# A fused attention, cosine feed-forward and soft mixture kernel: the logits' steps emitted between a slot's remainder and its cosine

## The chip, the cores and the metric

The kernel runs on one core of a Trainium2 chip. The metric is the time of one execution on the device in microseconds (us), the median of several runs. A profile is one execution recorded by the hardware profiler; its span runs from the first to the last instruction. PE is the matrix engine, PEld its weight loads, DVE the vector engine, ACT the scalar engine, POOL and SP the two engines that here mostly issue DMAs.

## The reference

Three layers follow each other on 4608 tokens of width 512. Only the second and third matter here.

```python
def _moe_ref(x, w_in, w_out):            # x: 4608 x 512, w_in: 512 x 2048
    h = x @ w_in
    g = h * np.cos(h)
    return (g @ w_out).astype(np.float32)

def _moe2_ref(x, phi, w1, w2):           # phi: 512 x 32 slots
    logits = x @ phi
    d = logits - logits.max(0, keepdims=True)
    d = np.exp(d)
    d /= d.sum(0, keepdims=True) + 1e-09
    slot_input = d.T @ x
    ...
    c = logits - logits.max(1, keepdims=True)
    c = np.exp(c)
    c /= c.sum(1, keepdims=True) + 1e-09
    return (c @ slot_out).astype(np.float32)
```

Ahead of this stands a linear attention (a product of k and v for each head, its product with q, and a normalization by the root mean square); its output is x.

## The kernel before, in words

The tokens are cut into ten blocks: blocks 0 to 7 have 512 tokens, blocks 8 and 9 have 256. `SMALL` is 8, `NB` is 10. The 2048 columns of `w_in` are cut into 16 pieces of 128, so a block has 16 slots, written (j, f). From block 8 on, two slots are worked as a pair.

A slot makes one tile of g = h cos h. `main` (L384) issues twelve matmuls (the operands are split into a high and a low part; three products of four pieces each) into one PSUM tile of the pool `ps_m`, which has three tiles. `cos_a` (L405) finds the turns on ACT (L410) and the remainder on DVE (L413). `cos_b` (L430) is the sine on ACT (L417), shifted to a cosine. `cos_c` (L446) multiplies it with h on DVE (L456), which is the last reader of the PSUM tile, and transposes the result on DVE (L475, or L463 in a pair) for the blocks whose slot products use DMA to regroup the rows (`regroup`, L508: DMAs issued by SP and POOL).

The first `w_out` product is never made: the logits come from g and the product of `w_out` and `phi`. `logits` (L523, matmuls L528) adds four slots at a time into one PSUM tile. Over the tokens, a running maximum and a running sum are kept, and A is the running sum of exponentials times g. For block j the steps are, in their order:

- the last `logits`, then `l_evac` (L545): the logits are copied from PSUM by DVE (L547);
- `l_add` (L550): four small matmuls spread them over the partitions (L555);
- `l_max` (L569): the maximum (L573) and a scaling (L574) on DVE, and the copy of the logits into a tile `ld` (L576);
- `l_cross` (L583): a matmul (L585) brings the maxima of the partitions together, and DVE takes their maximum (L586) and the new running maximum (`l_new`, L589: L592, L593, L595, L596);
- `l_exp` (L598): the exponentials on ACT into `ld` (L602), with their sum; the factor for the old sum (L611); the running sum on DVE (L612);
- `l_T` (L621): two transposes on PE, first of the exponentials, then of the copied logits (L629), and two copies by DVE (L631, L632);
- `slot_acc` (L654) and `slot_add` (L669): 16 matmuls d times g (L665), added to A on DVE (L674).

The order of everything is written out by hand. `PLAN` gives each step a slot. `at` puts a step in `side` (run behind `main` of that slot), `late` in `post` (behind `cos_a`), `end` in `fin` (behind `cos_c`), `ld_at` in `loads` (ahead of `main`). Steps in `amid` are run inside `main`, behind the fourth matmul (behind the eighth in block 8). Each engine works through its own instructions in the order of emission. `U(j, f)` turns a slot past 15 into one of the next block. For blocks 2 to 6 the last `logits` and `l_evac` are in slot 17 of block j, that is (j+1, 1), `l_add` and `l_max` in (j+1, 2), `l_cross` and `l_exp` inside `main` of (j+1, 3), `l_T` behind `main` of (j+1, 4) and `slot_acc` in (j+1, 6). For block 7 they are in (8, 1), (8, 2), (8, 3), (8, 5) and (8, 7). For block 0 `l_evac` is in (1, 14), `l_add` in (1, 15), `l_cross` in (2, 0); for block 1 they are in (2, 2), (2, 3) and (2, 4), with `l_T` in (2, 5) and `slot_acc` in (2, 6).

The loop from L1183 runs a slot as `loads`, `main`, `side`, `cos_a`, `post`, `cos_b`, `cos_c`, `fin`; the loop from L1192 does the same for pairs.

Of the kernel before, what the change touches and what calls it, by code (L numbers as in the profile page):

```python
# [8 lines left out]
F32 = mybir.dt.float32  # L9
# [17 lines left out]
    wq=(7, 10, 13, 15),  # L27
    l0=(9, 9, 12, 13, 15, 15, 17, 17),
    E=((18, 19, 3, 1), (18, 19, 3, 1)),
    F=((21, 22), (21, 22)),  # L30
    L=4,
    LI=2,
    PI=2,
# [11 lines left out]
    le=17,  # L45
    la=18,
# [18 lines left out]
NB = len(SIZES)  # L65
# [3 lines left out]
SMALL = SIZES.index(256)  # L69
# [3 lines left out]
def tile_linear_attention__ffn_cos__soft_moe(  # L73
# [13 lines left out]
    nc = tc.nc  # L87
    B, H, D = kv.shape[0], 8, 64
    NF, KD = w_in.shape[0], w_in.shape[2]
# [14 lines left out]
    ps_m = ctx.enter_context(tc.tile_pool(name="ps_m", bufs=PLAN["pm"], space=bass.MemoryType.PSUM))  # L104
# [279 lines left out]
    def main(j, f, ps=None):  # L384
        if ps is None:
            ps = ps_m.tile([128, 512], F32, tag="h", name="h")
        w, x = w_t[f], xt_t[j]
        assert all((j, t) in x_done for t in range(TT[j])) and ("S", f, 0) in done
        n = 0
        for kk in range(KD):  # L390
            for a, b in ((0, 0), (0, 1), (1, 0)):
                nc.tensor.matmul(out=ps, lhsT=w[:, a, kk, :], rhs=x[b][:, kk, :],  # L392
                                 start=(n == 0), stop=(n == 3 * KD - 1))
                n += 1
                if n == (8 if j == SMALL else 4):
                    run(amid, j, f)
        h_t[j, f] = ps

# [31 lines left out]
    def cos_b(j, f):  # L430
        cosine(fr_t[j, f])
# [86 lines left out]
                    in_=src[32 * x:32 * x + 32].rearrange("p (t b) f i -> p b t (f i)", b=4)[:, b],  # L518
                )

    l_t = {}

    def logits(j, c):  # L523
        if c == 0:
# [44 lines left out]
    def l_max(j):  # L569
        ps = lr_t[j]  # L570
        mb = sm_p.tile([128, 8], F32, tag="mb", name="mb")
        if j < SMALL:
            nc.vector.tensor_reduce(out=mb[:, 0:1], in_=ps[:, 0:128], axis=AX.X, op=ALU.max)  # L573
            nc.vector.tensor_scalar(out=mb[:, 4:8], in0=quarter, scalar1=mb[:, 0:1], scalar2=None, op0=ALU.mult)  # L574
            ld = one_p.tile([128, TB], F32, tag="ls", name="ld").rearrange("p (i t) -> p i t", t=128)[:, 0:2]
            nc.vector.tensor_copy(out=ld[:, 0], in_=ps[:, 0:128])  # L576
            lr_t[j] = (ps, mb, ld)
        else:
            nc.vector.tensor_reduce(out=mb[:, 0:1], in_=ps, axis=AX.X, op=ALU.max)
            lr_t[j] = (ps, mb, None)  # L580
            l_new(j)
# [16 lines left out]
    def l_exp(j):  # L598
        ps, mb, ld = lr_t.pop(j)
        sb = sm_p.tile([128, 2], F32, tag="sb", name="sb")  # L600
        if j < SMALL:
            nc.scalar.activation(out=ld[:, 1], in_=ps[:, 0:128], func=AF.Exp, bias=mb[:, 2:3], accum_out=sb[:, 0:1])  # L602
        else:
            ld = one_p.tile([128, TB], F32, tag="ls", name="ld")[:, 0:SIZES[j]]
            nc.scalar.activation(out=ld, in_=ps, func=AF.Exp, bias=mb[:, 2:3], accum_out=sb[:, 0:1])
            if j == NB - 1:
                ls_t[j] = ps
            else:
                nc.vector.tensor_copy(out=ld[0:32], in_=ps[0:32])
        if j:  # L610
            nc.scalar.activation(out=mb[:, 3:4], in_=mb[:, 1:2], func=AF.Exp)  # L611
            nc.vector.scalar_tensor_tensor(out=s_run, in0=s_run, scalar=mb[:, 3:4], in1=sb[:, 0:1],  # L612
                                           op0=ALU.mult, op1=ALU.add)
        else:
            nc.vector.tensor_copy(out=s_run, in_=sb[:, 0:1])
        ld_t[j] = ld
        sc_t[j] = mb

    ab_t = {}

# [307 lines left out]
    side = {}  # L928
# [6 lines left out]
    def late(j, f, fn, *a):  # L935
        post.setdefault((j, f), []).append((fn, a))
# [3 lines left out]
    def U(j, f):  # L940
        if j == 0 and f >= NF:
            j, f = 1, f - L
        return j + f // NF, f % NF
# [4 lines left out]
    def late2(j, f, *a):  # L948
        late(*U(j, f), *a)

    fin, amid = {}, {}

    def end(j, f, fn, *a):
        fin.setdefault((j, f), []).append((fn, a))
# [9 lines left out]
    for j in range(NB):  # L964
# [26 lines left out]
        if j < NB - 1:  # L991
            for c in range(4 * (j > 1)):
                at2(j, 4 * c + 7 if j == SMALL else PLAN["lg"][c], logits, j, c)
            le, la, lx, how = (PLAN["E"][j] if j < 2 else (19, 21, 5, 1) if j == SMALL
                               else (PLAN["le"], PLAN["la"], *PLAN["lx"]))
            at2(j, le, l_evac, j)
            at2(j, la, l_add, j)
            at2(j, la, l_max, j)
            if j < SMALL:
                amid.setdefault(U(j, la + 1), []).extend([(l_cross, (j,)), (l_exp, (j,))])  # L1000
            else:
                (at2, late2, end2)[how](j, NF + lx, l_exp, j)
        else:
            for c in range(3):
                at2(j, (7, 11, 14)[c], logits, j, c)
            at2(j, 14, l_evac, j)
            at2(j, 15, l_add, j)
            for f in range(12, NF):
                side.setdefault((j + (f + 2) // NF, (f + 2) % NF if f > 13 else 15), []).insert(0 if f > 13 else 99, (l_add, (j, f)))
            at2(j, 18, l_max, j)  # L1010
            at2(j, 18, warm, 5)
            end(NB, 3, l_exp, j)
            side[NB, 0].insert(0, (exp_table, ()))
# [43 lines left out]
    def run(d, j, f):  # L1057
        for fn, a in d.pop((j, f), []):
            fn(*a)

    wo2 = {}

# [93 lines left out]
    with tc.manual_schedule():  # L1156
# [24 lines left out]
            for t in (PLAN["one"] if f < L else PLAN["two"]).split():  # L1181
                token(t, f)
        for j, f in [(1, f) for f in range(NF - L, NF)] + [(j, f) for j in range(2, SMALL) for f in range(NF)]:  # L1183
            run(loads, j, f)
            main(j, f)
            run(side, j, f)
            cos_a(j, f)
            run(post, j, f)
            cos_b(j, f)
            cos_c(j, f)  # L1190
            run(fin, j, f)
        for j, f in [(j, f) for j in range(SMALL, NB) for f in range(0, NF, 2)]:  # L1192
            if (j, f) == (NB - 1, NF - 2):
                for i in range(2):
                    ps = ps_m.tile([128, 512], F32, tag="h", name="h")[:, 0:256]
                    run(loads, j, f + i)
                    main(j, f + i, ps)
                    run(side, j, f + i)
                    if i:
                        cos_b(j, f)  # L1200
                    cos_a(j, f + i)
                cos_c(j, f)
                cos_b(j, f + 1)
                cos_c(j, f + 1)
                continue
            ps = ps_m.tile([128, 512], F32, tag="h", name="h")
            for i in range(2):
                run(loads, j, f + i)
                main(j, f + i, ps[:, 256 * i:256 * i + 256])
                run(side, j, f + i)  # L1210
            h_t[j, f] = ps
            cos_a(j, f)
            for i in range(2):
                run(post, j, f + i)
            cos_b(j, f)
            cos_c(j, f)
            for i in range(2):
                run(fin, j, f + i)
# [71 lines left out]
```

## Time and profile before

| what | value |
|---|---|
| median of 3 runs | 674.75 us (673.41 to 674.92) |
| the profiled execution | 675.04 us |
| its span | 673.2 us |
| mean granted clock of PE, of full | 0.994 |
| busy PE, PEld | 643.4 us, 473.6 us |
| busy DVE, ACT, POOL | 492.6 us, 325.1 us, 208.7 us |
| read from and written to memory | 91.29 MB, 13.63 MB |

Busy is the time in which an engine works on an instruction, from the first to the last; matmuls are pipelined, so their modelled ends overlap, and a busy PE need not be at its peak. Time an engine spends waiting is put down to the instruction that ended the wait. An engine that is not the bottleneck may wait without cost.

### The profile page before, as it was taken

The numbers are of one execution on the slowest core, as the hardware profiler recorded it, in microseconds if no ns is written. First come the engines' busy times: TensorE is split into PE (matmuls) and PEld (weight loads), VectorE is DVE, ScalarE is ACT, GpSimd is POOL, SyncE is SP. The second block draws the span as 40 slices with busy tenths as digits, with TensorE's granted clock in tenths as the row PEclk, the third lists the DMA queues.
The fourth block names the chain that finished last, engine by engine and source line by source line (L and its number), as shares of the span: only waits on it lengthen the run. The fifth ranks groups of instructions, "written<-read, shape, count | busy, mean of one in ns | idle before, by whom it ended". The sixth has DMA issues, their size and how long they took to land.

```text
span 673.2 us, 12709 instructions
## 1 busy us (share of the span) xinstructions
PE 643.4 (96%) x4689; PEld 473.6 (70%) x4689; DVE 492.6 (73%) x927; ACT 325.1 (48%) x589; POOL 208.7 (31%) x291
## 2 busy tenths in 40 slices
PE   7889999999999999999999999999999999999993
PEld 6767787776557776777677677767667778984452
DVE  3899989966666778887888788787777756556243
ACT  3576767544344445445444554543463443553032
POOL 2451112310363443542543243335416322200000
PEclk9999999999999999999999999999999999999997
DMA  8955664212385636784788377575745369999998
GB/s 316 362 187 192 203 217 141 63 31 63 89 195 138 173 81 177 199 238 107 182 219 210 93 184 207 160 217 143 166 116 121 68 192 287 310 411 399 407 405 356
DMA packets 70589, 135.13 MB, mean 201 GB/s; under 512 B 10752, under 2 KB 39040, under 8 KB 69504
## 3 DMA queue, kind: packets, MB, share of 16 engines
q1 hardware_dynamic: 63360, 119.63, 55.5%
q0 software_dynamic: 7168, 14.69, 9.6%
q8 instruction: 37, 0.61, 0.4%
q14 instruction: 24, 0.20, 0.1%
HBM read 91.29 MB, written 13.63 MB: 156 GB/s over the span
## 4 chain that ended last, share of the span: by engine, by line
PE 75%; DVE 11%; DMA 5%; ACT 3%; issue 2%; POOL 1%; SPq 1%; DVEq 0%; ACTq 0%
PE h L392 47%; PE ab L665 5%; PE ops L203 4%; PE l L528 3%; DMA g<-tr 2%; DVE tmp L413 2%; PE eh L821 2%; PE eo L858 2%; PE kvps L184 2%; DVE gT L456 2%; DVE tr L475 2%; PE xTps L242 2%; ACT tmp L417 2%; PE l L537 2%; PE tr L497 2%
## 5 line engine op out<-in xcount | busy, mean ns | idle before, releaser
L392 PE MATMUL h<-xt,w 128*128 128x512 f32 (+1 forms) x1920 | 423.1, 374 | 2.4 <-POOL w L328 1.0
L392 PEld LDWEIGHTS h<-xt,w 128*128 128x128 f32 x1920 | 328.7, 189 | 84.2 <-issue 12.9
L417 ACT ACTIVATE tmp<-tmp,hpi 128x512 f32<-128x512 f32 (+1 forms) x145 | 104.2, 720 | 182.4 <-DVE tmp L413 182.2
L516 POOL DMA_DIRECT2D g<-tr x224 | 123.8, 555 | 119.6 <-DVE tr L475 47.1
L456 DVE TENSOR_TENSOR gT<-tmp,h 128x512 f32<-128x512 f32 x130 | 89.2, 686 | 68.3 <-ACT tmp L417 68.2
L217 POOL TENSOR_TENSOR ri<-ss,mhalf 128x8 f32<-128x8 f32 x36 | 59.5, 1656 | 188.1 <-DVE ss L215 178.6
L413 DVE SCALAR_TENSOR_TENSOR tmp<-h,tmp 128x512 f32<-128x512 f32 (+1 forms) x145 | 97.2, 674 | 23.7 <-ACT tmp L410 23.1
L410 ACT ACTIVATE tmp<-h 128x512 int32<-128x512 f32 (+1 forms) x145 | 85.2, 587 | 45.0 <-PE h L392 42.7
L475 DVE STREAM_TRANSPOSE tr<-gT 128x512 f32<-128x512 f32 x103 | 73.2, 711 | 6.9 <-DMA g<-tr 2.2
L328 POOL TENSOR_TENSOR w<-st_m,w 128x512 fp32r<-128x512 f32 x16 | 21.4, 1336 | 63.0 <-ACT w L323 63.0
L203 PE MATMUL ops<-kvA,q 128*128 128x128 f32 (+1 forms) x320 | 38.7, 279 | 0.1
L203 PEld LDWEIGHTS ops<-kvA,q 128*128 128x128 f32 (+1 forms) x320 | 34.5, 180 | 2.9 <-issue 1.9
L246 ACT ACTIVATE xt<-xTps,gn 128x512 fp32r<-128x512 f32 x36 | 24.5, 685 | 21.2 <-PE xTps L242 21.2
L665 PE MATMUL ab<-g,d 128*32 128x512 f32 x256 | 33.2, 593 | 1.4 <-DMA g<-tr 1.4
L528 PE MATMUL l<-gT,wp 128*32 128x512 f32 (+1 forms) x248 | 30.9, 556 | 0.0
L255 DVE SCALAR_TENSOR_TENSOR xt<-xTps,gn,xt 128x512 fp32r<-128x512 f32 x36 | 25.9, 728 | 4.1 <-ACT xt L246 4.0
L212 ACT ACTIVATE sq<-ops 128x512 f32<-128x512 f32 x31 | 18.4, 595 | 18.2 <-PE ops L203 18.2
L214 DVE TENSOR_REDUCE ss<-sq 128x8 f32<-128x512 f32 x31 | 21.1, 679 | 7.6 <-ACT sq L212 7.4
L665 PEld LDWEIGHTS ab<-g,d 128*32 128x32 f32 x256 | 10.0, 110 | 21.0 <-issue 19.1
L224 DVE TENSOR_TENSOR sq<-ops,ri 128x512 f32<-128x512 f32 x31 | 20.9, 676 | 1.2 <-POOL ri L217 1.2
L184 PEld LDWEIGHTS kvps<-kv 128*64 128x64 f32 x448 | 15.4, 137 | 8.7 <-issue 5.2
L242 PE MATMUL xTps<-ident,sq 128*128 128x128 f32 x124 | 18.9, 276 | 1.7 <-DVE sq L224 1.7
(205 smaller groups left out, 596.4 us busy)
## 6 DMA issues: line engine op xcount, KB each, us to landing
kv<-in_kv SPq DMA_DIRECT2D x28, 512.0 KB, 5.4
g<-tr SPq DMA_DIRECT2D x224, 64.0 KB, 4.0
g<-tr POOLq DMA_DIRECT2D x224, 64.0 KB, 4.0
ew<-in_ew SPq DMA_DIRECT2D x23, 512.0 KB, 9.0
q<-in_qT SPq DMA_DIRECT2D x36, 256.0 KB, 6.3
out<-ot SPq DMA_DIRECT2D x11, 768.0 KB, 6.5
rw<-in_w_in SPq DMA_DIRECT2D x16, 512.0 KB, 4.4
nat<-in_w_out SPq DMA_DIRECT2D x16, 512.0 KB, 4.1
```

The costliest lines, as they stand in the source:

```text
L203: nc.tensor.matmul(out=ps[p0:p0 + n, pr * 128:(pr + 1) * 128], lhsT=q_t[j, t][:, pr, p0:p0 + n], rhs=kvbd[b % 2][:, pr, :], start=True, st ...
L217: nc.gpsimd.tensor_tensor(out=ri[:, :, 0], in0=ss, in1=mhalf, op=ALU.pow)
L242: nc.tensor.transpose(ps[:, kk * 128:(kk + 1) * 128], xs[:, kk * 128:(kk + 1) * 128], ident)
L392: nc.tensor.matmul(out=ps, lhsT=w[:, a, kk, :], rhs=x[b][:, kk, :], start=(n == 0), stop=(n == 3 * KD - 1))
L410: nc.scalar.activation(out=t.bitcast(I32), in_=ps, func=AF.Copy, bias=0.25, scale=INV_2PI)
L413: nc.vector.scalar_tensor_tensor(out=t, in0=ps, scalar=INV_2PI, in1=t.bitcast(I32), op0=ALU.mult, op1=ALU.subtract)
L417: nc.scalar.activation(out=t, in_=t, func=AF.Sin, bias=hpi, scale=TWO_PI)
L456: nc.vector.tensor_tensor(out=g, in0=fr, in1=h_t.pop((j, f)), op=ALU.mult)
L475: nc.vector.transpose(out=tr_t[j, q][:, :, i, :], in_=gT_t[j, n * q + i].rearrange("p (b t) -> p b t", t=32))
L516: (nc.gpsimd if b % 2 else nc.sync).dma_start(out=dst[32 * b:32 * b + 32, :, x, a:a + n, :].rearrange("p t f i -> p t (f i)"), in_=src[32 ...
L528: nc.tensor.matmul(out=l_t[j][32 * o:32 * o + 32, :], lhsT=wp[:, f, :], rhs=gT_t.pop((j, f)), start=(c == 0), stop=(c == (2 if j == NB - 1 ...
L665: nc.tensor.matmul(out=ps[32 * c:32 * c + 32, :], lhsT=d[:, t, :], rhs=gs[c // 2][t][:, (c % 2) * 512:(c % 2) * 512 + 512], start=(t == 0) ...
```

## The change

The code of the next slot's `main` is emitted between `cos_a` and `cos_b` of the slot before, together with the logits' steps that belong to that next slot: `go` runs `loads` and `main` of a slot once, `go_next` does so for the slot that `nxt` names and takes the listed steps out of its `side`. For blocks 2 to 6 these are the last `logits` and `l_evac`, then `l_add` and `l_max`; for blocks 0 and 1 only `l_add` and `l_max`. `l_cross` stays inside `main` of the slot behind, now emitted ahead of the earlier slot's `cos_b`; `l_exp` follows that `cos_b`, and the new `l_sum` (the copy of the logits into `ld` and the running sum) follows its `cos_c`. For block 7, whose steps fall into pairs, `l_add` and `l_max` are emitted behind `cos_a` of pair (8, 0), with `main` of (8, 2) into a tile taken early; `l_cross` comes behind the twelfth matmul of `main` (8, 3), `l_exp` behind `cos_a` of pair (8, 2), `l_sum` behind its `cos_c`. `slot_acc` and `slot_add` of block 1 go from (2, 6) to (2, 7).

```diff
-    F=((21, 22), (21, 22)),
+    F=((21, 22), (21, 23)),
...
-                if n == (8 if j == SMALL else 4):
+                if n == (12 if j == SMALL else 4):
                     run(amid, j, f)
...
     def l_max(j):
...
-            nc.vector.tensor_copy(out=ld[:, 0], in_=ps[:, 0:128])
             lr_t[j] = (ps, mb, ld)
...
     def l_exp(j):
...
             if j == NB - 1:
                 ls_t[j] = ps
-            else:
-                nc.vector.tensor_copy(out=ld[0:32], in_=ps[0:32])
         if j:
             nc.scalar.activation(out=mb[:, 3:4], in_=mb[:, 1:2], func=AF.Exp)
+        sc_t[j] = mb
+        ld_t[j] = ld
+        lr_t[j] = (ps, sb)
+        if j >= SMALL:
+            l_sum(j)
+
+    def l_sum(j):
+        ps, sb = lr_t.pop(j)
+        ld, mb = ld_t[j], sc_t[j]
+        if j < SMALL:
+            nc.vector.tensor_copy(out=ld[:, 0], in_=ps[:, 0:128])
+        elif j < NB - 1:
+            nc.vector.tensor_copy(out=ld[0:32], in_=ps[0:32])
+        if j:
             nc.vector.scalar_tensor_tensor(out=s_run, in0=s_run, scalar=mb[:, 3:4], in1=sb[:, 0:1],
                                            op0=ALU.mult, op1=ALU.add)
         else:
             nc.vector.tensor_copy(out=s_run, in_=sb[:, 0:1])
-        ld_t[j] = ld
-        sc_t[j] = mb
...
             if j < SMALL:
-                amid.setdefault(U(j, la + 1), []).extend([(l_cross, (j,)), (l_exp, (j,))])
+                amid[U(j, la + 1)] = [(l_cross, (j,))]
+                e, a, x = (U(j, k) for k in (le, la, la + 1))
+                if j == SMALL - 1:
+                    late(*a, l_exp, j)
+                    end(*a, l_sum, j)
+                    nxt[a[0], a[1] - 2] = (a, j, (l_add, l_max), False)
+                else:
+                    for q, fns in ((e, (logits, l_evac)), (a, (l_add, l_max)), (x, ())):
+                        if q != e or j > 1:
+                            nxt[divmod(q[0] * NF + q[1] - 1, NF)] = (q, j, fns, q == x)
...
+    def go(j, f, ps=None):
+        if (j, f) not in ran:
+            run(loads, j, f)
+            main(j, f, ps)
+            ran.add((j, f))
+
+    def go_next(j, f, ps=None):
+        if (j, f) not in nxt:
+            return None
+        q, b, fns, last = nxt.pop((j, f))
+        go(*q, ps)
+        rest_ = []
+        for fn, a in side.pop(q, []):
+            if fn in fns and a[0] == b:
+                fn(*a)
+            else:
+                rest_.append((fn, a))
+        if rest_:
+            side[q] = rest_
+        return b if last else None
...
-            run(loads, j, f)
-            main(j, f)
+            go(j, f)
             run(side, j, f)
             cos_a(j, f)
             run(post, j, f)
+            b = go_next(j, f)
             cos_b(j, f)
+            if b is not None:
+                l_exp(b)
             cos_c(j, f)
+            if b is not None:
+                l_sum(b)
             run(fin, j, f)
...
-            ps = ps_m.tile([128, 512], F32, tag="h", name="h")
+            ps = pair_ps.pop() if pair_ps else ps_m.tile([128, 512], F32, tag="h", name="h")
             for i in range(2):
-                run(loads, j, f + i)
-                main(j, f + i, ps[:, 256 * i:256 * i + 256])
+                go(j, f + i, ps[:, 256 * i:256 * i + 256])
                 run(side, j, f + i)
             h_t[j, f] = ps
             cos_a(j, f)
             for i in range(2):
                 run(post, j, f + i)
+            if (j, f) in nxt:
+                pair_ps.append(ps_m.tile([128, 512], F32, tag="h", name="h"))
+                go_next(j, f, pair_ps[0][:, 0:256])
             cos_b(j, f)
             cos_c(j, f)
```

## Rows read from the trace of the kernel before

**Rows 1.** The page: busy time, share of the span and instructions of each engine.
```profile
PE 643.4 (96%) x4689; PEld 473.6 (70%) x4689; DVE 492.6 (73%) x927; ACT 325.1 (48%) x589; POOL 208.7 (31%) x291
```
**Rows 2.** Waits of PE: waiting line, releaser, us in total, times, longest.
```profile
PE lr L585 <- DVE ld L576: 3.9, 4, 1.2
...
PE ab L665 <- DMA g<-tr: 1.4, 1, 1.4
...
PE lr L555 <- DVE ls L547: 0.7, 1, 0.7
...
PE ldT L629 <- ACT ld L602: 0.4, 1, 0.4
```
**Rows 3.** Timeline, block 4's steps: start, length, engine, line, operation, [idle before <-releaser].
```profile
367.07 1.18 PE L392 MATMUL h<-xt,w 128*128 128x512 f32 x4
...
368.23 4.81 PE L392 MATMUL h<-xt,w 128*128 128x512 f32 x20
...
370.42 0.69 DVE L456 TENSOR_TENSOR gT<-tmp,h 128x512 f32<-128x512 f32 x1 [0.79 <-ACT tmp L417]
...
373.92 2.33 PE L392 MATMUL h<-xt,w 128*128 128x512 f32 x9
```
**Rows 4.** Timeline, PE around the L585 of block 0.
```profile
160.12 1.20 PE L392 MATMUL h<-xt,w 128*128 128x512 f32 x4
...
162.46 4.84 PE L392 MATMUL h<-xt,w 128*128 128x512 f32 x20
```
**Rows 5.** Timeline, slot products of blocks 0 and 1 and what follows each.
```profile
173.12 3.64 PE L665 MATMUL ab<-g,d 128*32 128x512 f32 x32
...
176.69 1.16 PE L203 MATMUL ops<-kvA,q 128*128 128x128 f32 x8
...
194.20 0.60 PE L665 MATMUL ab<-kv,d 128*32 128x512 f32 x2
...
200.44 5.75 PE L392 MATMUL h<-xt,w 128*128 128x512 f32 x24
```
**Rows 6.** Timeline, block 7's steps in block 8.
```profile
543.40 0.42 PE L555 MATMUL lr<-ls,rep 128*32 128x128 f32 x8
...
543.75 1.21 PE L392 MATMUL h<-xt,w 128*128 128x256 f32 x8
543.96 0.69 DVE L456 TENSOR_TENSOR gT<-tmp,h 128x512 f32<-128x512 f32 x1 [0.79 <-ACT tmp L417]
...
545.39 0.25 DVE L573 TENSOR_REDUCE mb<-lr 128x1 f32<-128x128 f32 x1
...
545.82 0.28 DVE L576 COPY ld<-lr 128x128 f32<-128x128 f32 x1
...
546.58 0.16 DVE L586 TENSOR_REDUCE mb<-lr 128x1 f32<-128x4 f32 x1 [0.48 <-PE lr L585]
...
547.20 1.28 ACT L602 ACT_TABLE_LOAD   x1 [3.27 <-DVE mb L595]
...
548.50 0.37 ACT L602 ACTIVATE ld<-lr,mb 128x128 f32<-128x128 f32 x1
...
548.95 0.59 ACT L410 ACTIVATE tmp<-h 128x512 int32<-128x512 f32 x1
...
549.97 3.12 PE L392 MATMUL h<-xt,w 128*128 128x256 f32 x24
...
551.60 0.69 DVE L456 TENSOR_TENSOR gT<-tmp,h 128x512 f32<-128x512 f32 x1 [1.34 <-ACT tmp L417]
552.32 0.71 DVE L463 STREAM_TRANSPOSE tr<-gT 128x512 f32<-128x512 f32 x1
552.96 0.25 DVE L631 COPY d<-ldT 128x128 f32<-128x128 f32 x1
```
**Rows 7.** Windows of 1 us: length, busy (instructions) per engine, granted clock, DMA share, GB/s.
```profile
663.00:664.00 1.00, 0.00 (x0) 0.00 (x0) 0.00 (x0) 0.00 (x0) 0.00 (x0) 1.00 1.05 436
...
665.00:666.00 1.00, 0.00 (x0) 0.00 (x0) 0.00 (x0) 0.00 (x0) 0.00 (x0) 0.50 1.03 424
```

More of the change, by code (lines that the diff above doesn't have):

```diff
@@ L519, in regroup @@
                 )
-    l_t = {}
+    l_t, pair_ps = {}, []
     def logits(j, c):
@@ L949, in late2 @@
         late(*U(j, f), *a)
-    fin, amid = {}, {}
+    fin, amid, nxt, ran = {}, {}, {}, set()
     def end(j, f, fn, *a):
```

## The prediction, made from these rows alone

> **What bounds the kernel now.** I read the busy shares first: PE is busy for 643.4 of 673.2 us, DVE for 492.6, ACT for 325.1 [rows 1]. PE sets the pace, so only a wait of PE's own is worth anything, and the second view is the list of what PE waited for [rows 2]. Of its idle time the steps named by the change hold four entries: the cross product of the maxima (L585) waits four times for DVE, 3.9 us in all; the slot product (L665) waits once for a regrouping DMA, 1.4 us; the replication of the logits (L555) waits once for DVE, 0.7 us; the transpose of the exponentials (L629) waits once for ACT, 0.4 us. The timeline shows the four L585 waits in blocks 0, 1, 6 and 7; in blocks 2 to 5 PE does not wait there.
>
> The idle entries understate the loss, because the matmuls' ends are modelled. So I price from start to start. In block 4 nothing is disturbed: from the first of four main matmuls to the resumption after L585 it is 368.23 - 367.07 = 1.16 us [rows 3]. In block 0 it is 162.46 - 160.12 = 2.34 us [rows 4]: that wait costs 1.18 us, not the 0.9 that idle time shows. A slot product takes 176.69 - 173.12 = 3.57 us undisturbed; that of block 1 took 200.44 - 194.20 = 6.24 us, so it lost 2.67 us [rows 5].
>
> Why PE waits at L585: its input is the end of a row on DVE. DVE runs about a slot behind PE, and in its order the cosine's multiply (0.69 us) and transpose (0.71 us) of the slot before stand ahead of the maximum, and the copy of the logits (0.28 us) behind it is waited for too; block 7 shows it [rows 6].
>
> **The change, part by part.** *The order on PE* stays: the next slot's main product came next anyway, and the logits' steps stood right behind it. SP and POOL keep their order too: the next slot's loads (regrouping DMAs among them, four issues on each queue per slot) are emitted earlier, but only past the sine, the multiply and the transpose, which put nothing on those queues. So this part moves DVE and, in block 7, ACT.
>
> *Evacuation and maximum ahead of the multiply* (blocks 0 to 6; in 0 and 1 the maximum alone). For the three L585 waits in blocks 0, 1 and 6 the input comes 0.69 + 0.71 + 0.28 = 1.68 us sooner, against a loss of 1.18 each: they go, 3 x 1.18 = 3.5 us. The lower bound is the idle time, 3.9/4 = 0.98 each, 2.9 us. The evacuation before the multiply also takes block 6's L555 wait (0.7 us), and the exponential earlier takes block 3's L629 wait (0.4 us), whose DVE chain comes out about 1 us earlier. The added wait: DVE now holds evacuation, maximum and cross maximum until the next main product has passed, and the multiply, transpose and next remainder queue behind. Who would notice is PE, for the PSUM tile that the multiply frees (three tiles: slot f+3 needs slot f's). In block 4 the multiply of slot 2 starts at 370.42, ends at 371.11, and slot 5's product starts at 373.92, a slack of 2.8 us [rows 3]. DVE also sat idle 0.79 us before that multiply, waiting for the sine; an evacuation or maximum that fits there costs nothing. I take zero; the upper bound is a rival below.
>
> *Copy and running sum behind the transpose.* Blocks 0 to 6 transpose the exponentials a whole main product later, so the copy is hidden by it.
>
> *The second slot product one slot later.* A main product goes in front of it. Block 1's DMA comes out of a chain that starts at block 0's slot product, so it moves up with block 0's 1.18 us, while PE arrives 2 x 1.18 earlier and then spends a main product of at most 2.9 us (24 matmuls take 5.75 [rows 5]). That leaves 0 to 0.4 us of wait; if the DMA does not move at all, 1.5 us. Gain 2.67 less 0.3: 2.4 us, bounds 1.2 and 2.67.
>
> *Block 7* is emitted differently and here I expect a loss. The exponential goes behind the turns of pair (8,2) and ahead of its sine; the copy goes behind that pair's transpose; the L629 transposes stay behind main (8,5), and the second of them needs the copy. From [rows 6]:
> - the replication ends at 543.40 + 0.42 = 543.82; maximum and scaling take 0.43 (545.39 to 545.82), so the multiply of (8,0) starts at 544.25, and from multiply to the next thing after its transpose it is 545.39 - 543.96 = 1.43: 545.68. The cross product, now after twelve matmuls from 543.75, is done by then (eight took 1.21).
> - from the cross maximum to the table load 547.20 - 546.58 = 0.62: 546.30. From that table load to the multiply 551.60 - 547.20 = 4.40, less the turns (0.60) that now stand ahead: 3.80, so the multiply starts at 550.10. It and the transpose take 552.96 - 551.60 = 1.36, the copy 0.28: 551.74.
> - the second transpose follows, and main (8,6) starts about 0.2 later, near 551.95. Before, it started at 549.97 [rows 6].
> So block 7 ends 2.0 us later than before, with its own L585 wait already gone: PE would reach the transposes at about 548.7 and sit there for 3 us. Bounds: 1.8, if the table is loaded while ACT still waits, and 2.6, if nothing overlaps.
>
> One rule speaks against this part. The row shows the table load at 547.20 for 1.28 us and the exponential at 548.50, so a switch costs 1.30 us and two of them lie in the 3.80 [rows 6]. The Trainium skill ("ScalarE: Activation LUTs", What ACT_TABLE_LOAD costs) puts a drain of some 1.38 us beside each load, 2.66 us a switch. By the page block 7 would lose 2.0 + 2.8 = 4.8 us and the whole would come to 672.6 us; the trace shows no such drain, and I go by it.
>
> **The sum.** 3.5 + 0.7 + 0.4 + 2.4 = 7.0 us gained before block 8, 2.0 given back in it: 5.0 us. The profiled execution took 675.04 us, 1.84 more than its span of 673.2, and lies 0.29 above the median of 674.75. I subtract from the median: 669.75, say **669.8 us**. The tail should follow: its transfers fill all DMA engines (share 1.03 and more [rows 7]), but they start when PE frees weight and slot tiles in blocks 8 and 9, so they start 5.0 us earlier as well.
>
> **Rivals.**
> *No loss in block 7.* If the copy is not what the transposes wait for, or DVE reaches it before PE arrives, the 2.0 us stay, and block 7's own L585 wait is gained: 543.75 to 549.97 is 6.22 us for 36 matmuls that take 36 x 3.12/24 = 4.7 and some 0.4 for the cross product, so 1.1 us. 669.8 - 3.1 = 666.7. Against it stands the emission order: the copy is behind a sine that is behind two table loads.
>
> *The waits come back elsewhere.* PE waits for DVE, DMA and ACT by turns [rows 2]; a PE that is earlier may meet the next one, first of all block 1's DMA: with the lower bounds, 2.9 for L585, 1.2 for the slot product, 0.5 of the two small ones, less 2.6 in block 7, 2.0 is left, so 672.7 us, the edge of no change; with only half of that 673.7.
>
> *The tiles come back too late (slower).* Three DVE steps in a row each wait for a main product. It decides from the point at which the multiply of slots 0 to 2 ends more than the 2.8 us of slack later [rows 3]; from there each us is one of PE in every block that has the new order, seven times. An overrun of 1.2 us gives 7 x 1.2 = 8.4: 678.2 us. For it: DVE is at 73% and a slot behind. Against: the evacuation fits into idle time DVE has anyway, and each wait is for something PE finished about when DVE gets there.
>
> *The clock.* Behind PE's last matmul, from 663 to 664, PE had nothing to do and the granted clock was still full; from 665 to 666 it was at half, 1.2 GHz [rows 7]. The 3 us of idle that I expect in block 7 come near to that. If the clock falls there, the two main products behind (3.12 us [rows 6]) take 3.1 us longer, and the slot product and what follows may too: 673 to 676, take 673.5. The Trainium skill ("TensorE: Matmul & The Clock Gate", What's actually happening) also has the engine at half rate after idling; the end of this trace agrees.
>
> *Dearer switches.* If ACT lost about as much again behind each of the two table loads, 1.3 us by the row's own 1.30, the loss in block 7 grows by 2.6: 672.4. The rows speak against it: the exponential starts 0.02 us after the load ends [rows 6]. By the page it would be the 672.6 given above.
>
> **How the numbers follow.** The forecast as argued: 0.60, its own range 668.3 to 671.8. No loss in block 7: 0.08. Waits come back: 0.12. Clock: 0.08. Dearer switches: 0.03. Tiles too late: 0.09. The range leaves out the tiles and most of the no-loss case: 667.0 to 674.0. A measurement of this kernel tells 0.3% from no change, 2.0 us: faster means under 672.7. That holds for nearly all of the forecast, the no-loss case and a part of the waits case: 0.70; the clock, the dearer switches and the rest of the waits give 0.20 within; the tiles case and the worst of the clock give 0.10 slower.
>
> **What would show it.** In PE's waits after: no L585 entry; no or under 0.5 us for L665; a new entry of about 3 us for L629 behind DVE's copy, near 545 us of the new span, with main (8,6) close behind. DVE's copy of the logits stands behind (8,2)'s transpose. PE's waits for DVE's multiply stay as small as before in slots 3 to 6; if they grow to whole us in every block, the tiles rival is right. No L629 wait in block 7 would make my loss wrong, and an L665 wait above 1 us the gain of the later slot product. A granted clock under 1.00 behind the L629 wait shows the clock rival.

## The result, and the profile after

The kernel after takes 669.05 us (median of 6 runs, 667.93 to 669.44) against 674.47 us before (6 runs, 673.41 to 675.81): a ratio of 0.9916 [0.9904, 0.9929], 5.4 us faster. Forecast were 669.8 us. The profiled execution took 667.93 us, the fastest of the six, with a span of 666.1 us.

The page of the kernel after, busy time, share and instructions of each engine, answers to [rows 1]:

```profile
PE 639.8 (96%) x4689; PEld 473.5 (71%) x4689; DVE 493.3 (74%) x927; ACT 325.5 (49%) x589; POOL 208.8 (31%) x291
```

The work is the same; PE's busy time, which holds some hidden waiting, is 3.6 us less. Of the four entries in [rows 2] none is left under the new line numbers (L584 is the cross product, L674 the slot product, L555 the replication), but the transposes (now L638) have a new one. Waits of PE in the kernel after: waiting line, releaser, us in total, times, longest:

```profile
PE ldT L638 <- DVE ld L619: 3.1, 1, 3.1
...
PE h L392 <- DVE gT L456: 0.3, 1, 0.3
```

The second row matters too: PE's wait for the multiply, through which a late PSUM tile would show, is 0.3 us once, as before.

The timeline of PE in the kernel after, at the cross product of block 0 (first two rows, against [rows 4]) and at the slot product of block 1 (the others, against [rows 5]):

```profile
160.26 1.19 PE L392 MATMUL h<-xt,w 128*128 128x512 f32 x4
161.43 4.82 PE L392 MATMUL h<-xt,w 128*128 128x512 f32 x20
...
192.16 3.02 PE L392 MATMUL h<-xt,w 128*128 128x512 f32 x12
195.11 0.62 PE L674 MATMUL ab<-kv,d 128*32 128x512 f32 x2
...
198.68 3.02 PE L392 MATMUL h<-xt,w 128*128 128x512 f32 x12
```

From the four main matmuls to the resumption it is now 161.43 - 160.26 = 1.17 us, the undisturbed 1.16 of [rows 3]. The slot product has a main product in front and takes 198.68 - 195.11 = 3.57 us: all of the 2.67 is back.

Block 7 in the kernel after, against [rows 6] (timeline: start, length, engine, line, operation, idle before and its releaser):

```profile
536.05 1.70 PE L392 MATMUL h<-xt,w 128*128 128x256 f32 x12
...
538.46 1.28 ACT L601 ACT_TABLE_LOAD   x1
539.76 0.37 ACT L601 ACTIVATE ld<-lr,mb 128x128 f32<-128x128 f32 x1
...
540.33 1.28 ACT L417 ACT_TABLE_LOAD   x1
540.68 0.27 PE L638 MATMUL ldT<-ident,ld 128*128 128x128 f32 x1
...
541.62 0.72 ACT L417 ACTIVATE tmp<-tmp,hpi 128x512 f32<-128x512 f32 x1
...
542.37 0.69 DVE L456 TENSOR_TENSOR gT<-tmp,h 128x512 f32<-128x512 f32 x1 [3.01 <-ACT tmp L417]
543.10 0.71 DVE L463 STREAM_TRANSPOSE tr<-gT 128x512 f32<-128x512 f32 x1
543.73 0.25 DVE L619 COPY ld<-lr 128x128 f32<-128x128 f32 x1
...
544.04 0.33 PE L638 MATMUL ldT<-ident,ld 128*128 128x128 f32 x1 [3.09 <-DVE ld L619]
544.12 3.12 PE L392 MATMUL h<-xt,w 128*128 128x256 f32 x24
...
544.40 0.29 DVE L640 COPY d<-ldT 128x128 f32<-128x128 f32 x1 [0.30 <-PE ldT L638]
...
547.62 3.81 PE L674 MATMUL ab<-g,d 128*32 128x512 f32 x32
551.37 6.02 PE L392 MATMUL h<-xt,w 128*128 128x256 f32 x48
```

This is the chain that was forecast: two table loads, the sine, the multiply, the transpose, and only then the copy that the second transpose wants. From main (8,3) to main (8,6) it is 544.12 - 536.05 = 8.07 us, 549.97 - 543.75 = 6.22 before: a loss of 1.85. But the next row gives something back. The slot product of block 7 took 558.25 - 553.47 = 4.78 us before:

```profile
553.47 4.85 PE L665 MATMUL ab<-g,d 128*32 128x512 f32 x32
558.25 6.01 PE L392 MATMUL h<-xt,w 128*128 128x256 f32 x48
```

It takes 551.37 - 547.62 = 3.75 after: 1.03 us less. What it lost before against an undisturbed product, 4.78 - 3.57 = 1.2 us, has no idle entry, and it was no wait for a regrouping DMA. The regrouping DMAs of block 7 in the kernel before (view of the tile g: issues with the first and the last start, then the time from issue to landing):

```profile
L516 SPq DMA_DIRECT2D g<-tr x8: 585/606/640, 541.5 to 546.1; - x8
...
DMA to landing us min/median/max: 2.2/2.7/3.3
```

The last was issued at 546.1 and landed at most 3.3 us later, 4 us ahead of the product. What came late was the other operand, `d`: before, DVE's copy of it ended at 552.96 + 0.25 = 553.21 [rows 6], 0.26 ahead of the product, since the multiply and the transpose of pair (8, 2) stood in front of it. After, these two are done before the second transpose on PE, and the copy ends at 544.40 + 0.29 = 544.69, 2.93 ahead. All thirteen profiles of this document agree: where the copy ends 0.2 to 0.3 us ahead of block 7's slot product (before, e1, e4 to e7), the product takes 4.65 to 4.78 us; where it ends 1.9 us ahead or more (the others), 3.53 to 3.75. Why a product so close behind its copy takes 1.1 us longer is not shown.

**A ledger of four parts** serves for all kernels below. It is cut at rows of PE's timeline: the start (until the 11 main matmuls of the first product, 23.59 before), the body (from there to main (8,2)), block 7 (from main (8,3) to the L563 of block 8, 543.75 to 581.29 before), the tail (from there to the end of the profiled execution). What lies between body and block 7 is 1.97 to 1.99 us everywhere.

```
kernel                     start   body  block 7  tail  profiled execution
before                     23.59 518.19  37.54   93.75  675.04
after                      23.78 510.30  38.36   93.52  667.93
after, second profile      25.54 510.47  38.20   94.50  670.70
e1 copy first              23.37 510.29  36.01   93.82  665.47
e2 ... and slot later      24.23 511.01  35.18   93.76  666.16
e2 again (e11)             24.63 510.51  35.18   94.22  666.52
e3 slot back               23.59 513.46  39.61   93.80  672.43
e4 slot alone              23.84 515.97  37.53   93.61  672.93
e5 copy later alone        25.28 517.17  37.22   93.68  675.33
e6 block 7 as before       23.88 510.92  37.39   93.79  667.97
e7 order alone             24.39 513.50  37.52   94.33  671.73
e8 wait filled too long    23.79 511.49  40.32   94.19  671.77
e9 wait filled             24.43 510.91  38.22   93.88  669.42
```

From before to after (the first profile) the body gained 7.9 us, block 7 lost 0.8 net, the tail followed. Eight rows have the body of the kernel after, without a change in it (after twice, e1, e2 twice, e6, e8, e9): they lie between 510.29 and 511.49 us, so the gain of the body is 6.7 to 7.9 us, and a difference under 1 us between two bodies says little.

### The profile page after: what moved, and what is told of

The parts are those of the page before. It is cut to its first block, busy times and chain, and to the rows that moved or that the text cites. A ratio compares the mean times of both kernels' runs of the same rounds, so it can differ in the third digit from the quotient of the medians.

```text
span 666.1 us, 12705 instructions
## 1 busy us (share of the span) xinstructions
PE 639.8 (96%) x4689; PEld 473.5 (71%) x4689; DVE 493.3 (74%) x927; ACT 325.5 (49%) x589; POOL 208.8 (31%) x291
## 4 chain that ended last, share of the span: by engine, by line
PE 87%; DVE 5%; DMA 2%; ACT 2%; issue 1%; POOL 0%; SPq 0%; DVEq 0%; ACTq 0%
PE h L392 57%; PE ab L674 4%; PE ops L203 4%; PE l L528 4%; PE kvps L184 2%; PE eh L830 2%; PE eo L867 2%; PE xTps L242 2%; PE l L537 2%; PE tr L497 2%; DMA ew<-in_ew 1%; DMA kv<-in_kv 1%; PE fo L896 1%; DVE tmp L413 1%; PE wps L340 1%
## 5 line engine op out<-in xcount | busy, mean ns | idle before, releaser
L674 PE MATMUL ab<-g,d 128*32 128x512 f32 x256 | 31.2, 593 | 0.0
L674 PEld LDWEIGHTS ab<-g,d 128*32 128x32 f32 x256 | 9.4, 110 | 16.1 <-issue 14.5
```

Source lines behind the costliest of these rows:

```text
L674: nc.tensor.matmul(out=ps[32 * c:32 * c + 32, :], lhsT=d[:, t, :], rhs=gs[c // 2][t][:, (c % 2) * 512:(c % 2) * 512 + 512], start=(t == 0) ...
```

## The experiments

**e1, the copy first.** The kernel after, with block 7's copy of the logits back in `l_max`.

```diff
     def l_max(j):
...
+            if j == SMALL - 1:
+                nc.vector.tensor_copy(out=ld[:, 0], in_=ps[:, 0:128])
...
     def l_sum(j):
...
-        if j < SMALL:
+        if j < SMALL - 1:
             nc.vector.tensor_copy(out=ld[:, 0], in_=ps[:, 0:128])
-        elif j < NB - 1:
+        elif SMALL <= j and j < NB - 1:
...
```

> The changed kernel, but block 7's copy of the logits stands behind its maximum again and no longer behind the transpose of pair (8,2). Theory (the copy is what the second transpose waits for): PE's 3.1 us wait at the transposes goes, and from main (8,3) to main (8,6) it takes 5.1 us instead of 8.07. Then PE meets block 7's regrouping DMA about 3 us sooner, and its slot product, 3.75 us from start to start in the changed kernel and 4.78 in the kernel before, grows to some 5.6: about 1.1 us are left, 668 us. Rival 1 (no DMA wait behind it): the slot product stays at 3.75 and all 3.0 us stay, 666.1 us. Rival 2 (the transposes wait for the exponentials and their table loads): the wait stays, 669 us.

Measured: 666.22 us (665.47 to 667.13), ratio 0.988 [0.9862, 0.9898]. The timeline of PE and DVE in this kernel:

```profile
535.64 1.70 PE L392 MATMUL h<-xt,w 128*128 128x256 f32 x12
...
540.27 0.38 PE L640 MATMUL ldT<-ident,ld 128*128 128x128 f32 x2
540.41 3.12 PE L392 MATMUL h<-xt,w 128*128 128x256 f32 x24
...
543.42 0.28 DVE L642 COPY d<-ldT 128x128 f32<-128x128 f32 x1
...
543.91 4.76 PE L676 MATMUL ab<-g,d 128*32 128x512 f32 x32
548.61 6.01 PE L392 MATMUL h<-xt,w 128*128 128x256 f32 x48
```

Both transposes run in one group and main (8,6) comes 4.77 us after main (8,3), not 8.07: the wait is the copy's place alone. The slot product takes 548.61 - 543.91 = 4.70 us again, 1.1 more than undisturbed and not the 2 that the theory set. The theory's reason was wrong, too: in the view of the tile g the last regrouping DMA was issued at 538.0 and landed at most 3.3 us later, 2.6 us ahead of the product, but the copy of `d` ends at 543.42 + 0.28 = 543.70, 0.21 ahead of the product. Block 7 gains 2.35 net.

**e2, and the slot product a main product later.** e1, with `slot_acc` of block 7 behind main (8,8); a weight load that takes over a tile of block 7 moves one slot too.

```diff
-        lT, sa = (PLAN["F"][j] if j < 2 else (22, 23) if j == NB - 1 else (21, 23) if j == SMALL - 1
+        lT, sa = (PLAN["F"][j] if j < 2 else (22, 23) if j == NB - 1 else (21, 24) if j == SMALL - 1
...
-    ld_at(8, 8, fill, g_p, "g1", 8)
+    ld_at(8, 9, fill, g_p, "g1", 8)
```

> As the run with the copy first, and block 7's slot product one slot later, behind main (8,8); the load into the tile that it reads moves one slot with it. Theory (the DMA behind the wait): the main product in front (1.6 us) takes up most of what the slot product would wait, which then takes some 4.0 us, 666.4 us. Rival 1 (no DMA wait there): nothing gained by the later slot, same time as the run with the copy first.

Measured: 665.92 us (665.59 to 666.57), ratio 0.9872 [0.9857, 0.9887]. The timeline of PE and DVE in this kernel:

```profile
545.00 0.28 DVE L642 COPY d<-ldT 128x128 f32<-128x128 f32 x1
...
545.60 1.69 PE L392 MATMUL h<-xt,w 128*128 128x256 f32 x12
547.22 3.64 PE L676 MATMUL ab<-g,d 128*32 128x512 f32 x32
550.79 4.58 PE L392 MATMUL h<-xt,w 128*128 128x256 f32 x36
```

The product is undisturbed (3.57): with a main product in front it starts 547.22 - 545.28 = 1.94 us behind the copy of `d`. The landings under e1 rule the DMA out as what the later slot saves. Block 7 is 0.83 shorter than in e1 by the ledger. The medians differ by 0.3 only, inside the spread of both; that e2 beats e1 is shown for the stage, not for the whole.

**e6, block 7 as before.** The kernel after, with block 7's steps where they were: cross product, exponential and running sum behind the eighth matmul of main (8,3), the copy in `l_max` (by the edits of e1, which belong to it).

```diff
-                if n == (12 if j == SMALL else 4):
+                if n == (8 if j == SMALL else 4):
...
                 if j == SMALL - 1:
-                    late(*a, l_exp, j)
-                    end(*a, l_sum, j)
-                    nxt[a[0], a[1] - 2] = (a, j, (l_add, l_max), False)
+                    amid[x] += [(l_exp, (j,)), (l_sum, (j,))]
```

> The changed kernel with block 7 handled as in the kernel before: maximum in side of (8,2), cross product and exponential inside main (8,3) behind the eighth matmul, copy behind the maximum; blocks 0 to 6 and the later second slot product as changed. Theory: from main (8,3) to main (8,8) it took 14.50 us before and 15.32 after, so block 7's part of the change is a net loss of about 0.8 us: 668.2 us, with the L585 wait of about 1.2 us back in block 7 and the slot product at about 4.8 us. Rival (block 7's part is worth something by itself, its L585 wait being gone): slower than the changed kernel, 670 us or more.

Measured: 667.48 us (667.31 to 667.97), ratio 0.9895 [0.988, 0.991]: below the 668.2 expected. One L586 wait of 1.2 us is back, the 3.1 us are gone, and block 7 takes 37.39 us. So block 7's part of the change is a loss of 0.8 to 1.0 us in the profiles and 1.6 in the medians (669.05 - 667.48, of runs that were not made side by side); without it the change would be better.

**e3, the slot product back.** The kernel after, with block 1's `slot_acc` in (2, 6) again.

```diff
-    F=((21, 22), (21, 23)),
+    F=((21, 22), (21, 22)),
```

> The changed kernel with block 1's slot product back in slot (2,6). Theory: PE arrives 2.26 us sooner than before (two L585 waits gone) while the DMA it waits for comes only about 1.2 us sooner, since it follows block 0's slot product: the slot product takes about 7.3 us from start to start instead of 3.57, 3.7 us more, 672.7 us. Rival (the DMA moves with PE): 6.24 us as before, 2.7 us more, 671.7 us.

Measured: 672.43 us (671.02 to 674.42), ratio 0.9974 [0.9961, 0.9988]. The timeline of PE at the product:

```profile
191.90 0.60 PE L674 MATMUL ab<-kv,d 128*32 128x512 f32 x2
...
195.37 0.59 PE L674 MATMUL ab<-g,d 128*32 128x512 f32 x1 [2.43 <-DMA g<-tr]
...
198.89 5.74 PE L392 MATMUL h<-xt,w 128*128 128x512 f32 x24
```

In the kernel before the wait ended here:

```profile
196.91 0.59 PE L665 MATMUL ab<-g,d 128*32 128x512 f32 x1 [1.38 <-DMA g<-tr]
```

The product takes 6.99 us, more than the 6.24 of before: PE comes 2.3 us earlier (191.90 against 194.20), the DMA only 1.54 (195.37 against 196.91). The body is 3.16 us longer than that of the kernel after, which fits the 3.4 us between the medians; in this one execution block 7 is 1.25 us longer as well, for another reason (under e8 and e9).

**e4, the later slot product alone,** and **e7, the new order alone.** e4 is the kernel before with this line:

```diff
-    F=((21, 22), (21, 22)),
+    F=((21, 22), (21, 23)),
```

e7 is e6 with the line turned round:

```diff
-    F=((21, 22), (21, 23)),
+    F=((21, 22), (21, 22)),
```

> The kernel before with block 1's slot product one slot later, and nothing else of the change. Theory (priced from start to start): the DMA lands near 196.9 us, the main product in front lasts until about 197.1, so the wait is gone and the slot product takes 3.57 us instead of 6.24: 2.7 us less, 671.7 us. Rival (priced by the idle entry): 1.4 us less, 673.0 us.

> The changed kernel with block 7 handled as in the kernel before and block 1's slot product back in slot (2,6): what is left is the new order of blocks 0 to 6. Theory: 1.17 + 1.09 + 1.27 for three L585 waits, 0.73 and 0.60 for the two small ones, 4.9 us, less 0.75 because block 1's slot product waits longer when PE arrives sooner (6.99 against 6.24 us): 4.1 us less than before, 670.2 us. Rival (the parts add up without acting on each other): 669.5 us.

Measured: e4 672.66 us (671.75 to 673.83), ratio 0.9971 [0.9958, 0.9984], its slot product 3.57 us; e7 671.02 us (669.96 to 674.14), ratio 0.9949 [0.9933, 0.9966], its slot product 7.09. Both gain less than their theories: e4 674.61 - 672.66 = 1.95 us in the median, not 2.7 (PE's waits for the multiply rose from 0.3 to 0.7 us in it), e7 674.61 - 671.02 = 3.59, not 4.1. In the ledger's body e4 gains 2.22 us and e7 4.69, together 6.91; the eight bodies with both parts gain 6.7 to 7.9. That the parts help each other is shown at the product: an earlier PE alone loses 0.75 to 0.85 us more there than before. The sums fit that, but hardly go beyond their scatter; in the medians e6, which has just these two parts, gains 6.86 us, and e4 and e7 add up to 5.54.

The later slot product does not always escape the DMA. In five of the eight profiles with this body block 1's product takes 3.57 us, and the last DMA for it had landed 0.3 to 0.6 us before its start. In e2, e6 and e8 the last one landed 0.1 to 0.9 us behind the start, and the product took 3.91, 4.02 and 4.76 us. The slowest of these DMAs took 6.8, 7.0 and 7.7 us from issue to landing there, 6.2 to 6.5 in the five. The timeline of PE in e8:

```profile
195.13 0.62 PE L676 MATMUL ab<-kv,d 128*32 128x512 f32 x2
...
196.36 0.59 PE L676 MATMUL ab<-g,d 128*32 128x512 f32 x1 [0.18 <-DMA g<-tr]
...
199.89 3.03 PE L392 MATMUL h<-xt,w 128*128 128x512 f32 x12
```

An idle entry of 0.18 us stands here for a loss of 4.76 - 3.57 = 1.19.

**e5, the copy later alone.** The kernel before, with the copy of blocks 0 to 7 emitted behind the exponential.

```diff
     def l_max(j):
...
-            nc.vector.tensor_copy(out=ld[:, 0], in_=ps[:, 0:128])
             lr_t[j] = (ps, mb, ld)
...
     def l_exp(j):
...
             nc.scalar.activation(out=ld[:, 1], in_=ps[:, 0:128], func=AF.Exp, bias=mb[:, 2:3], accum_out=sb[:, 0:1])
+            nc.vector.tensor_copy(out=ld[:, 0], in_=ps[:, 0:128])
```

> The kernel before with the copy of the logits of blocks 0 to 7 emitted behind the exponential instead of behind the scaling, and nothing else. Theory (the cross product waits for the copy too, since it writes into the same PSUM tile): each of the four L585 waits shrinks by the copy's part of about 0.2 us, 3.9 us to some 3.1, 673.6 us. Rival (it waits for the scaling alone): the four waits stay at 3.9 us, 674.4 us.

Measured: 673.75 us (672.18 to 675.33), ratio 0.9986 [0.9972, 0.9999]. Waits of PE in this kernel:

```profile
PE lr L584 <- DVE mb L574: 3.2, 4, 1.0
...
PE ab L665 <- DMA g<-tr: 0.5, 1, 0.5
```

The four waits fall from 3.9 to 3.2 and now name the scaling: the cross product had also waited for the copy, which stands behind the scaling in DVE's queue and reads the PSUM tile that the cross product writes. The rest of each wait is the multiply and the transpose ahead. The second row, 0.5 instead of 1.4, comes of a faster DMA in this execution; it returns below.

**e8 and e9, the wait filled.** The profile of e3 shows the clock rival at work. Windows of 1 us of e3 (length, busy of PE, PEld, DVE, ACT, POOL, granted clock, DMA share, GB/s), behind a wait that ends at 547.01:

```profile
547.00:548.00 1.00, 0.99 (x8) 0.99 (x9) 0.70 (x4) 0.00 (x0) 0.00 (x0) 1.00 0.93 246
...
549.00:550.00 1.00, 1.00 (x7) 1.00 (x6) 0.71 (x2) 0.22 (x1) 0.00 (x0) 0.50 1.10 387
...
552.00:553.00 1.00, 1.00 (x20) 0.31 (x12) 0.69 (x1) 0.27 (x1) 0.00 (x0) 1.00 0.99 426
```

PE was back at work for more than a microsecond at a full clock, then the clock fell, to half from 549 on, and was full again from 552. Main (8,6) with main (8,7), 3.12 us elsewhere, took longer (timeline of PE in e3):

```profile
547.10 4.48 PE L392 MATMUL h<-xt,w 128*128 128x256 f32 x24
```

In the kernel after the same stretch, behind a wait as long, ran at a full clock (windows as above):

```profile
545.00:546.00 1.00, 1.00 (x11) 1.00 (x9) 0.49 (x1) 0.47 (x1) 0.00 (x0) 1.00 1.02 287
546.00:547.00 1.00, 1.00 (x11) 1.00 (x9) 0.69 (x1) 0.25 (x1) 0.00 (x0) 1.00 0.83 270
```

Could that be why the profiled executions differ by 7.1 us (675.04 to 667.93) and the medians by 5.4? e8 and e9 are the kernel after, with the wait filled by matmuls whose result nobody reads.

```diff
     def l_T(j):
...
             for i in (1, 0):
                 nc.tensor.transpose(bank[:, 128 * i:128 * i + 128], ld[:, i], ident)
+                if i and j == SMALL - 1:
+                    warm(24)        # e9: warm(13)
```

> The changed kernel with 24 matmuls of the identity, 128 columns each and used by nobody, between block 7's two transposes, so that PE works while it would wait for the copy. Theory (the clock falls behind that 3.1 us wait in some of the executions and costs 1.4 us each time, as in the profile of the run with the slot back): 668.3 us, 0.3 to 1.4 under the changed kernel, and a granted clock of 1.00 from 530 to 600 us. Rival (the clock plays no part in the changed kernel's median): 669.0 us, or a little more if the extra matmuls outlast the wait.

e8 missed its design. Measured: 671.48 us (670.63 to 672.88). The timeline of PE in e8:

```profile
542.00 5.52 PE L801 MATMUL warm<-ident 128*128 128x128 f32 x48
```

24 such matmuls are 48 records and outlast the wait by over 2 us, so e8 tells nothing of the clock. From this row e9 was cut to 13, and the kernel after (e10) and e2 (e11) ran again, unchanged, beside it on the same chip.

> The kernel after with 13 extra matmuls of 128 columns (their result is used by nothing) between block 7's two transposes; 48 records of such took 5.5 us, so these take about 3.0 us and fill the 3.1 us for which PE waits for the copy, without outlasting it. Theory (the granted clock falls in a part of the executions behind that wait, and this is why the medians differ by 5.4 us where the profiled executions differ by 7.1): the median falls below that of the kernel after, by 0.5 us or more, to 668.5 or less. Rival (the clock behind the wait hardly weighs; the profiled execution was only one of the fastest): equal to the kernel after within 0.3 us, 668.9 to 669.3, or slightly slower if the extra work runs over.

> The kernel after once more, on the chip that runs the other two. Theory: 669.0 in the median again, with a spread of some 1.5 us, and 7.7 us earlier than before at main (8,2) in the profile. Rival (the first profile was an exceptional execution): that profile shows a wait or a lower clock that the first did not have, and its gain over before is nearer 5 us.

> The kernel with block 7's copy of the logits first and its slot product one slot later, once more, beside the kernel after on the same chip. Theory (the 3.1 us wait and the slot product's wait for its DMA are gone): 665.9, that is 3.1 us faster than the kernel after, outside the spread of both. Rival (the earlier difference came of different chips): under 2 us.

Measured: e9 668.97 us (668.18 to 669.61), ratio 0.9913 [0.9897, 0.9929]; the kernel after 669.54 (667.92 to 671.49), 0.9923 [0.9902, 0.9943]; e2 666.23 (665.91 to 666.52), 0.9873 [0.9855, 0.9892]. The timeline of PE in e9:

```profile
542.05 3.07 PE L801 MATMUL warm<-ident 128*128 128x128 f32 x26
545.31 0.33 PE L638 MATMUL ldT<-ident,ld 128*128 128x128 f32 x1 [0.19 <-DVE ld L619]
```

The wait is filled to 0.19 us. e9 lies 0.57 us below its neighbour, but not under the 668.5 that the theory asked for, and the spreads overlap: inconclusive. What differs between executions of the kernel after is elsewhere. Its second profile kept a full clock behind the wait and still took 2.77 us longer than the first: by the ledger 1.76 at the start, 0.98 in the tail, nothing in between. One window of 4 us in the start, in the first profile and then in the second:

```profile
8.00:12.00 4.00, 3.46 (x86) 3.27 (x83) 0.00 (x0) 1.66 (x8) 0.00 (x0) 1.00 1.05 384
```

```profile
8.00:12.00 4.00, 3.99 (x80) 3.96 (x80) 0.00 (x0) 1.24 (x6) 0.00 (x0) 0.57 1.05 389
```

There the granted clock was 0.57 in the mean, long before anything that the change touches; PE had just waited 1.96 us in one piece for an input (kv), against 1.07 in the first profile. So of e10's expectations the rival is right about a lower clock and about the whole gain, 675.04 - 670.70 = 4.3 us. Main (8,2) came 541.78 - 536.01 = 5.8 us earlier than before, not 7.7; only counted from the first product on, in the body, it is 518.19 - 510.47 = 7.7.

Does such a late start cost the kernel before less, because its wait for block 1's DMA takes some of it up? e5, which shares with it the place of block 1's slot product, looks like it: it began 1.69 us later (25.28), its slot product 195.56 - 194.20 = 1.36 later, and the DMA that ends the wait came only 0.45 later. But e7, with the same body as e3, began 0.80 later than e3, its product 0.81 and the DMA 0.91 later: nothing was taken up. What differs in e5 is the DMA itself, 6.1 us from issue to landing for the slowest, against 7.2 in before. So the theory of the late start is not borne out. The gap between 7.1 and 5.4 is one between single executions and medians: the profiled execution of before lies 0.57 above its median, that of after 1.12 below. Single executions are seen to differ by the start (up to 2.2 us), by the clock behind the wait (1.25) and by block 1's DMA (up to 1.2); what each does to the medians is open.

e11 settles the best version: e2 is 669.54 - 666.23 = 3.3 us faster than the kernel after on the same chip, with no overlap.

## Why the prediction was right

**What bounds the kernel: right.** PE does; the body became shorter by what PE no longer waits.

**The L585 waits: right, and the size.** Forecast 3 x 1.18 = 3.5 us, by start-to-start rows instead of idle time. Measured 1.17 (block 0), 1.09 (block 1, from 183.89 - 181.63 = 2.26 to 181.75 - 180.58 = 1.17) and 1.27 (block 6, from 490.52 - 488.09 = 2.43 to 482.83 - 481.67 = 1.16): 3.53. The idle entries would have given 2.9. e5 shows the copy's share of the cause, e7 that the new order removes the rest.

**L555 and L629: right.** 0.7 was forecast and 0.73 measured for block 6; 0.4 and 0.60 for block 3, where the entry again understated it.

**The later slot product: right, 2.67 for 2.4.** In both profiles of the kernel after the whole loss went. The 0.3 us kept back for a late DMA was right to keep: in e2, e6 and e8, which have the same body, 0.3 to 1.2 us of loss are left.

**The loss in block 7: right, 1.85 for 2.0, at the forecast place.** PE was to sit there for 3 us and did for 3.09. e1 proves the cause: with the copy first, the wait is gone. The rival of the dearer switches falls, too: from each table load to the activation behind it are 539.76 - 538.46 = 1.30 and 541.62 - 540.33 = 1.29 us, and the second load starts 0.20 us behind the end of the exponential (539.76 + 0.37 = 540.13). The Trainium skill ("ScalarE: Activation LUTs", What ACT_TABLE_LOAD costs) puts a drain of about 1.38 us beside such a load; these rows leave no room for it.

**What the sum missed.** Block 7's slot product returned 1.03 us. The prediction priced block 1's by start to start but took block 7's as undisturbed, since it has no entry among the waits; the same subtraction there, 4.78 against 3.57, would have shown a loss of 1.2 us, and its own rows show the copy of `d` right ahead of the product, in the queue that the change reorders. The terms before block 8 came to 3.53 + 0.73 + 0.60 + 2.67 = 7.5, for a forecast of 7.0, and main (8,2) came 541.78 - 534.08 = 7.7 us earlier. So the profiled execution gained 7.1 where the sum says 5.0. The median gained 5.4, and 674.53 - 669.54 = 5.0 in the repetition (e10), near the forecast. By the parts, 7.5 less the 0.8 of block 7, some 6.7 us were due; why the medians show less is not settled. That 669.8 is so close to 669.05 is in part luck.

**The rivals.** *No loss in block 7* is refuted by the 3.1 us. *The waits come back* did not come at the size that the rival set, but the mechanism is real: without the later slot product (e3, e7) block 1's product takes 0.75 to 0.85 us more than before, and with it the DMA is still late in some executions (e2, e6, e8). *The tiles come back too late* is refuted: the wait for the multiply stayed at 0.3 us, and in block 4 of the kernel after the multiply of slot 2 and the product of slot 5 are

```profile
365.22 0.69 DVE L456 TENSOR_TENSOR gT<-tmp,h 128x512 f32<-128x512 f32 x1
...
368.73 3.01 PE L392 MATMUL h<-xt,w 128*128 128x512 f32 x12
```

368.73 - 365.22 - 0.69 = 2.8 us of slack, as in [rows 3]: the steps fit into DVE's idle time. *The clock* happens: one of three profiles with the 3.09 us wait shows it, at a price of 1.25 us in block 7 (39.61 against 38.36), less than the 3.1 and more that the rival assumed, since the clock came back before the slot product. The Trainium skill ("TensorE: Matmul & The Clock Gate", What's actually happening) has the engine at half rate after idling; behind this wait one profile of three agrees, and two show a full clock throughout. How often it falls is open.

## What to carry to other kernels

Where one engine sets the pace, price a wait from the start of the work ahead to the start of the work behind, against an undisturbed place of the same kind, and do it for every product, also where no wait is listed; then look which operand came last before naming the cause. Ask of each step that moves with a group whether it has to: the copy alone, left behind the transpose, cost 3 us at PE, and putting it first made the kernel 3 us faster. Waits on PE and the transfers behind them are coupled, so measure the parts of a change alone and together, and see how much equal code scatters: here 2.2 and 4.7 us alone, 6.7 to 7.9 together in the same stretch.

## What was not expected of the hardware

The granted clock fell after PE had resumed from a 3.09 us wait and worked for over a microsecond at full clock, in one execution, and not in two others with a wait as long. The start of the kernel differs from one execution to the next by up to 2.2 us (23.37 to 25.54 in the ledger); in the second profile of the kernel after the clock was 0.57 from 8 to 12 us. The slowest regrouping DMA around block 1's slot product took 5.5 us from issue to landing in one profile (e4) and 7.7 in another (e8). And a loss can hide in a busy line: 1.2 us in a slot product with no idle entry, whose DMAs had landed 4 us before, and 1.19 us behind an idle entry of 0.18.
